# Attention and two mixture-of-experts layers on one core: casts, spare matmuls and scatters moved in a planned order

## Chip, cores and metric

The kernel runs on one core of a Trainium2 chip. The metric is the device time of one execution in microseconds; lower is better. All arithmetic that counts is float32: a matrix is split into a rounded high part and a low part (the rest), and a product is made of three TensorE passes (high by high, high by low, low by high).

## What is computed

```python
def reference(q, k, v, f, moe..., moe2...):         # cut
    scores = q @ k.T / sqrt(64) + decay(cumsum(log f)), causal   # 2 x 8 heads, 576 x 576, head size 64
    x = softmax(scores) @ v                                      # -> 1152 tokens x 512
    # first experts: two modalities, expert = argmax(x @ w_gate + bias[modality]), 8 experts, none dropped
    x = gate * (relu(x @ w1[e]) @ w2[e])                         # 512 -> 1024 -> 512
    # second experts: expert = argmax(x @ w_gate2), at most `capacity` (288) tokens each
    return gate * (relu(x @ w1[e]) @ w2[e])
```

## The kernel before

Nothing is left to a compiler's order. Every step is an `op` of a `Sched` (engine, an estimated duration, a priority, the buffers it reads and writes), and `Sched.run` makes a list schedule from the estimates: it takes whatever can start earliest by the plan, of operations within 0.02 us the one with the least priority, among those whose priority is within a window of the least one that is still to do. Steps marked `fill` (the casts of weights in attention) are put afterwards into gaps of the plan that are long enough. The instructions are then issued in the order of the plan. Each engine works through its own queue strictly in order, and semaphores make it wait for data; so an operation that the plan put too early blocks everything behind it on its engine. The plan's estimates are `PAR` and the numbers in the `op` calls, not the trace.

The stages, with the places that the change touches:

- **Attention**, 16 heads, `head` (L517 on), a planned period of 7.25 us. SP loads q, k and v (`load`, L496). TensorE transposes q and k (L519, L557), makes the scores in groups (L620 to L624), transposes the exponentials (L660), multiplies with v (L693) and turns the result (L717). ScalarE does the exponentials (L642) and the high parts, VectorE the row maxima (L634) and the low parts. Two strings of small VectorE operations, `consts5` (L835 to L843, it ends with a register for SP, which names the first experts to load) and `consts6` (L850 to L868), prepare the routing; each is one `op` with one estimate (0.7 and 1.2 us).
- **First weights**: from the planned time 54.7 us on, SP loads nine chunks of 512 KB (`chunk`, L359) into attention. Of the first four chunks ScalarE makes the high halves (L352) and GpSimd the low halves (L361), as `fill`; the plan lets a cast start when it believes that the load has landed.
- **Idle filler**: `busy` puts up to six matmuls of 128 columns (L1100) ahead of a TensorE operation that is late in the plan, up to the planned time 30 us.
- **First experts**: `route` makes the table of the tokens on VectorE, `tables` the lists, GpSimd gathers rows (L1195). The usual case has two experts of five blocks of 128 tokens. Casts of weights (`Region.split`) are on ScalarE (high) and VectorE (low, L361), and of every 16 low halves two (`plo`) are on GpSimd; four of the eight right after attention (`eplo`) and three of those before the second experts (`eplo2`) are on GpSimd too.
- **Second experts**, `experts()`: for each of the 8 experts a block of 128 tokens, and a second block under `tc.If`, if there are more. Two gathers (L2027) bring the rows, TensorE transposes them (L2035), makes the first product (L2092 to L2094), transposes the hidden layer (L2117), and makes the second product (L2143 to L2145). VectorE scales the result (L2166), GpSimd scatters it to `out` (L2173). Scatters into `out` wait for each other. The scatter of block (0,0) stands on GpSimd's queue ahead of the gathers of expert 1; in the last expert, as in all, block 0 comes ahead of block 1.

Of the kernel before, what the change touches and what calls it, by code (L numbers as in the profile page):

```python
# [13 lines left out]
ALU = mybir.AluOpType  # L14
AX = mybir.AxisListType
# [52 lines left out]
class Sched:  # L68
# [4 lines left out]
    def __init__(self):  # L73
        self.ops, self.slots, self.rings, self.banks = [], {}, 0.0, set()
# [50 lines left out]
    def commit(self, o, t, end):  # L125
# [21 lines left out]
    def run(self, window, slack=0.02, lat=0.18, margin=0.05, free=None, emit=True, busy=None):  # L147
# [11 lines left out]
        while len(order) < len(main):  # L159
# [20 lines left out]
            free[o["eng"]] = t + o["dur"]  # L180
            if busy is not None and o["eng"] == "PE" and t > last:
# [29 lines left out]
        if emit:  # L211
            for t, _, i in order:
                if "idle" in ops[i]:
                    busy(t, *ops[i]["idle"])
                ops[i]["fn"]()
# [8 lines left out]
def kernel(  # L224
# [608 lines left out]

    def consts5():
        vec.tensor_reduce(out=gm, in_=mb, axis=AX.X, op=ALU.max)  # L835
        vec.tensor_tensor(out=ge, in0=mb, in1=gm[:, :, None].to_broadcast([P, 2, E]), op=ALU.is_equal)
        vec.tensor_tensor(
            out=ge, in0=ge, in1=erev[:, :, 0][:, None, :].to_broadcast([P, 2, E]), op=ALU.mult
        )
        vec.tensor_reduce(out=gm, in_=ge, axis=AX.X, op=ALU.max)  # L840
        vec.tensor_tensor(out=go, in0=ge, in1=gm[:, :, None].to_broadcast([P, 2, E]), op=ALU.is_equal)
        vec.tensor_scalar(out=gif, in0=gm, scalar1=-1.0, scalar2=float(E), op0=ALU.mult, op1=ALU.add)
# [5 lines left out]
    def consts6():  # L848

        vec.tensor_tensor(out=g_1, in0=go[:, 0], in1=go[:, 1], op=ALU.mult)  # L850
        vec.tensor_tensor(out=g_1, in0=go[:, 1], in1=g_1, op=ALU.subtract)
        vec.tensor_tensor(out=g_x, in0=go[:, 0], in1=g_1, op=ALU.add)
        vec.tensor_scalar(out=gbig, in0=g_x, scalar1=131072.0, scalar2=None, op0=ALU.mult)
        vec.tensor_scalar(out=g_x, in0=g_x, scalar1=-1.0, scalar2=1.0, op0=ALU.mult, op1=ALU.add)
        vec.tensor_scalar(out=soff, in0=g_x, scalar1=131072.0, scalar2=None, op0=ALU.mult)
        vec.scalar_tensor_tensor(
            out=soff, in0=g_1, scalar=float(NJ * P), in1=soff, op0=ALU.mult, op1=ALU.add
        )
        vec.tensor_copy(out=capf, in_=capi[:, 0:1])
        vec.tensor_scalar(out=capl, in0=capf, scalar1=float(NB2 * P), scalar2=None, op0=ALU.min)  # L860
        vec.tensor_copy(out=idf[:, 1], in_=idi[:, :, 0])
        vec.tensor_scalar(out=idf[:, 0], in0=idf[:, 1], scalar1=-1.0, scalar2=1.0, op0=ALU.mult, op1=ALU.add)
        for m, t in ((0, btok), (1, bt1)):
            vec.tensor_tensor(
                out=t, in0=mb[:, m, :, None].to_broadcast([P, E, TT]),
                in1=idf[:, m, None, :].to_broadcast([P, E, TT]), op=ALU.mult,
            )
        vec.tensor_tensor(out=btok, in0=btok, in1=bt1, op=ALU.add)  # L868
# [165 lines left out]
    a5 = sc.op(D_, 0.7, consts5, prio=c_p0, after=[a1, a4], late=1.0)  # L1034
    a6 = sc.op(D_, 1.2, consts6, prio=c_p0 + T, after=[a3, a5])
# [60 lines left out]
    def busy(t, idle, o):  # L1096

        if t < par["wf1"]:
# [3 lines left out]
    est = sc.run(window=par["window"], free={"SP": 4.1, A_: 6.9, D_: 7.2, "POOL": 5.0}, emit=not par.get("only"), busy=busy)  # L1102
# [60 lines left out]
    class Region:  # L1163


        def __init__(self, two=False):
            self.sc = Sched()
            for n, t in (
                ("h", hps), ("ht", [htps]), ("ht2", [htps, ytps]),
                ("y", yps), ("yl", yps[1:2]), ("y0", yps[0:1]), ("x", [xps, htps] if two else [xps]), ("yt", [ytps]), ("lg", [rps[:, 504:504 + E]]),  # L1170
# [130 lines left out]
        def leave(self, blk, o, dst, second, y=None):  # L1301

            b_l, HD = Buf(None), DM // 2
            if y is not None:
                gate_ = [
                    (A_, 0.27, lambda: nc.scalar.mul(out=o.ap[:, 0:HD], in_=y[:, 0:HD], mul=gsl)),
                    (D_, 0.33, lambda: V.tensor_scalar(
# [5 lines left out]
            if second:  # L1313
# [18 lines left out]
                else:  # L1332
# [3 lines left out]
                    for u, (e, d) in enumerate(((A_, 0.27), (D_, 0.33))):  # L1336
# [105 lines left out]
        def single(self, blk, ie, slot, dst, second, pend=None, half=0, hold=None, deps=(), step=2, u=0, cond=None, later=False):  # L1442
# [5 lines left out]
            use, sb, hts = [], [], "ht" if second else "ht2"  # L1448
# [24 lines left out]
            def turn(i):  # L1473
                t, b = Buf(hts), Buf(None)
# [67 lines left out]
    def route(rg, lgt, pad, eoff, lim, nm, deps=(), shift=None):  # L1542
# [7 lines left out]
        def v(fn, r, dur=0.153, eng=D_):  # L1550
# [265 lines left out]
    rg = Region(True)  # L1816
# [6 lines left out]
    rg.split_load(range(KD, NCH), NCH, plo=par["eplo"])  # L1823
# [185 lines left out]
    def experts():  # L2009
# [11 lines left out]

        def rows(e, u):
# [8 lines left out]
            rg.op("POOL", 1.1, fn, w=[g], late=par["glate"], prio=p_ - 6.0)  # L2031
# [44 lines left out]
        class Block:  # L2076
# [83 lines left out]
            def leave(self, prio, o=None):  # L2160
                blk = bl2[self.e][self.u]
                if o is None:
# [135 lines left out]
```

## Time and profile before

| what | value |
|---|---|
| three timed runs | 495.01, 498.13, 501.61 us (median 498.13) |
| the profiled execution | 497.49 us, of which the span from its first to its last instruction is 495.7 us |
| mean granted TensorE clock | 0.964 of full speed |

The profile's rows come from that one execution. "Busy" is the time in which an engine had an instruction of the program; idle time stands in square brackets with what ended it. The clock column is the TensorE clock that was granted: 1.00 is 2.4 GHz and 0.50 is 1.2 GHz.

### The profile page before, as it was taken

The numbers are of one execution on the slowest core, as the hardware profiler recorded it, in microseconds if no ns is written. First come the engines' busy times: TensorE is split into PE (matmuls) and PEld (weight loads), VectorE is DVE, ScalarE is ACT, GpSimd is POOL, SyncE is SP. The second block draws the span as 40 slices with busy tenths as digits, with TensorE's granted clock in tenths as the row PEclk, the third lists the DMA queues.
The fourth block names the chain that finished last, engine by engine and source line by source line (L and its number), as shares of the span: only waits on it lengthen the run. The fifth ranks groups of instructions, "written<-read, shape, count | busy, mean of one in ns | idle before, by whom it ended". The sixth has DMA issues, their size and how long they took to land. (4 is left out here: it accounts for less than half of the span.)

```text
span 495.7 us, 8168 instructions
## 1 busy us (share of the span) xinstructions
PE 442.6 (89%) x2719; PEld 373.6 (75%) x2719; DVE 320.3 (65%) x684; ACT 270.9 (55%) x602; POOL 157.8 (32%) x190
## 2 busy tenths in 40 slices
PE   7878998899999879999889999897999999999950
PEld 6667887789888777988789977676887678778730
DVE  6797885598896774512771145776656999598320
ACT  6765785798776521502641116356567986497120
POOL 8741312555400512200330005133333283332100
PEclk9998999599999989999999999998999999999995
DMA  7462489997200552411291002417674879550000
GB/s 165 71 142 71 99 137 177 250 285 211 84 24 25 162 214 65 182 53 45 62 306 59 21 23 87 140 50 265 207 242 160 279 247 332 202 196 9 30 23 3
DMA packets 72694, 66.97 MB, mean 135 GB/s; under 512 B 45597, under 2 KB 54813, under 8 KB 72625
## 3 DMA queue, kind: packets, MB, share of 16 engines
q1 hardware_dynamic: 66448, 55.96, 39.3%
q0 software_dynamic: 4992, 10.08, 6.4%
q8 instruction: 25, 0.41, 0.4%
q10 hardware_dynamic: 1200, 0.30, 0.3%
q14 instruction: 29, 0.23, 0.2%
HBM read 58.62 MB, written 11.87 MB: 142 GB/s over the span
## 5 line engine op out<-in xcount | busy, mean ns | idle before, releaser
L2173 POOL DMA_INDIRECT out_dram<-mo,mo x16 | 18.6, 1165 | 79.1 <-DVE mo L2166 41.3
L352 ACT CAST mo<-wb 128x512 fp32r<-128x512 f32 x68 | 39.9, 633 | 4.9 <-PE yps L2145 4.6
L361 DVE TENSOR_TENSOR mo<-wb,mo 128x512 fp32r<-128x512 f32 x53 | 39.7, 777 | 3.8 <-ACT mo L352 3.0
L693 PE MATMUL one<-at,at 128*128 128x64 f32 (+2 forms) x192 | 36.4, 330 | 3.0 <-ACT at L642 1.7
L642 ACT ACTIVATE at<-one,at 128x512 f32<-128x512 f32 (+1 forms) x64 | 33.7, 532 | 8.3 <-DVE at L634 8.1
L352 ACT CAST wa<-wa 128x512 fp32r<-128x512 f32 x56 | 31.8, 623 | 7.8 <-DMA wa<-in_moe_w_dram 7.5
L361 DVE TENSOR_TENSOR wa<-wa,wa 128x512 fp32r<-128x512 f32 x42 | 33.4, 842 | 3.4 <-ACT wa L352 3.4
L693 PEld LDWEIGHTS one<-at,at 128*128 128x128 f32 x192 | 29.3, 194 | 6.5 <-DVE at L671 1.5
L2107 ACT ACTIVATE mo<-hps 128x512 f32<-128x512 f32 x30 | 17.7, 607 | 25.6 <-PE hps L2094 22.1
L671 DVE TENSOR_TENSOR at<-one,at 128x320 fp32r<-128x320 f32 (+1 forms) x32 | 17.6, 556 | 21.0 <-ACT at L667 20.4
L620 PE MATMUL one<-at,at 128*128 128x512 f32 (+1 forms) x64 | 26.6, 417 | 4.2 <-ACT at L709 4.2
L2143 PE MATMUL yps<-mo,wb 128*128 128x512 f32 x72 | 29.0, 402 | 0.6
L2145 PE MATMUL yps<-mo,wb 128*128 128x512 f32 x72 | 28.5, 396 | 0.9 <-DVE wb L2134 0.9
L660 PE MATMUL big<-ident,at 128*128 128x128 f32 x128 | 26.3, 280 | 3.4 <-DVE at L531 3.2
L1351 POOL DMA_INDIRECT x_d<-mo,mo x8 | 8.2, 1024 | 65.4 <-DVE mo L1348 47.8
L2144 PE MATMUL yps<-mo,wb 128*128 128x512 f32 x72 | 28.4, 394 | 0.0
L361 DVE TENSOR_TENSOR mo<-mo,mo 128x512 fp32r<-128x512 f32 x33 | 25.9, 823 | 2.7 <-ACT mo L352 2.7
L634 DVE TENSOR_REDUCE at<-one 128x1 f32<-128x512 f32 (+1 forms) x64 | 27.3, 474 | 0.4 <-PE one L624 0.4
L361 POOL TENSOR_TENSOR mo<-wb,mo 128x512 fp32r<-128x512 f32 x15 | 19.9, 1334 | 19.9 <-ACT mo L352 15.5
L2166 DVE TENSOR_SCALAR mo<-yps,mo 128x512 f32<-128x512 f32 x15 | 11.0, 741 | 23.3 <-PE yps L2145 23.3
L588 POOL TENSOR_TENSOR at<-at,at 128x320 fp32r<-128x320 f32 x16 | 13.9, 870 | 34.0 <-ACT at L577 33.9
L660 PE MATMUL one<-ident,at 128*128 128x128 f32 x112 | 23.4, 281 | 1.4 <-ACT at L642 1.4
(390 smaller groups left out, 1320.5 us busy)
## 6 DMA issues: line engine op xcount, KB each, us to landing
wb<-in_moe_w_dram SPq DMA_DIRECT2D x34, 512.0 KB, 5.2
wa<-in_moe_w_dram SPq DMA_DIRECT2D x28, 512.0 KB, 5.7
mo<-in_moe_w_dram SPq DMA_DIRECT2D x18, 512.0 KB, 5.4
at<-in_q_dram SPq DMA_DIRECT2D x30, 128.0 KB, 4.2
x_d<-zero SPq DMA_DIRECT2D x1, 2340.0 KB, 19.7
at<-in_k_dram SPq DMA_DIRECT2D x16, 128.0 KB, 4.5
at<-in_v_dram SPq DMA_DIRECT2D x16, 128.0 KB, 3.3
x_d<-at SPq DMA_DIRECT2D x8, 256.0 KB, 2.3
```

Source lines behind the costliest of these rows:

```text
L352: nc.scalar.copy(out=half(hi, u), in_=half(rt, u))
L361: lambda u, eng: eng.tensor_tensor(out=half(lo, u), in0=half(rt, u), in1=half(hi, u), op=ALU.subtract),
L620: nc.tensor.matmul(o, q1.ap[:, s0:s0 + n], k1.ap[:, a:e], start=True, stop=False)
L634: nc.vector.tensor_reduce(out=nm.ap[0:n], in_=ps.ap[0:n, c:c + w], axis=AX.X, op=ALU.max, negate=True)
L642: nc.scalar.activation(out=p.ap[0:n, 0:w], in_=ps.ap[0:n, c:c + w], func=AF.Exp, bias=nm.ap[0:n], scale=1.0, accum_out=st.ap[0:n, i:i + 1],)
L660: nc.tensor.transpose(out=t.ap[:, c:c + P], in_=ptile[i].ap[:, j * P:(j + 1) * P], identity=ident)
L693: nc.tensor.matmul(dst.ap[:, qa - off:qb - off], vt.ap[:, j].rearrange("p a d -> p (a d)"), ph[a][u].ap[:, ca:ca + qb - qa], start=(first ...
L2107: nc.scalar.activation(out=self.s.ap[:, 4 * i:4 * i + 4, :], in_=self.h[i].ap.rearrange("p (c t) -> p c t", t=P), func=AF.Relu,)
L2143: nc.tensor.matmul(self.y.ap, a, wh, start=(c == 0), stop=False)
L2144: nc.tensor.matmul(self.y.ap, a, wl, start=False, stop=False)
L2145: nc.tensor.matmul(self.y.ap, b, wh, start=False, stop=(c == KF - 1))
L2173: nc.gpsimd.indirect_dma_start(out=out, out_offset=blk.at(), in_=o.ap[:, 0:DM], in_offset=None, bounds_check=N - 1, oob_is_err=False,)
```

## The change

Six edits. (1) `consts5` and `consts6` become chains of single operations of 0.2 us with later priorities (4 and 5 periods instead of 1 and 2). (2) In the planned times 24 to 42 us, one matmul of 512 columns is put ahead of a TensorE operation whenever 2.4 us have gone by since the last such one. (3) The weight loads in attention count as landing 5 us later in the plan, and their low halves move from GpSimd to VectorE. (4) All other low halves are on VectorE too (`plo`, `eplo`, `eplo2` are empty), and right after attention those of chunks 6 and 7 wait for the list of rows. (5) The first scatter of the second experts waits for the first two gathers. (6) The last expert does its block 1 first and ends with block 0, whose result is scaled in two halves on ScalarE and VectorE. Estimates and offsets of the plan change beside these, and transposes of the hidden layer share two banks with those of the rows.

```diff
@@ Sched.run @@
+            if pace is not None and o["eng"] == "PE" and pace[0] < t < pace[1] and t > self.paced + pace[2]:
+                idle = [s for c in self.banks for s in self.slots[c] if s[2] is None and s[1] + lat < last]
+                if idle:
+                    s = min(idle, key=lambda s: s[1])
+                    self.paced, o["pace"] = t, s[0]
+                    t = max(t, last + 0.22)
...
-                end[o["n"]] = self.rings + 0.95
+                end[o["n"]] = self.rings + 0.95 + o["late"]
@@ attention @@
-    a5 = sc.op(D_, 0.7, consts5, prio=c_p0, after=[a1, a4], late=1.0)
-    a6 = sc.op(D_, 1.2, consts6, prio=c_p0 + T, after=[a3, a5])
+    def chain(steps, prio, after):
+        for fn in steps:
+            after = [sc.op(D_, 0.2, fn, prio=prio, after=after)]
+        return after
+    a5 = sc.op(D_, 0.2, consts5, prio=par["c5"] * T, after=chain(steps5, par["c5"] * T, [a1, a4]), late=1.0)
+    (a6,) = chain(steps6, par["c6"] * T, [a3, a5])
...
             "SP", 0.5, lambda m=m: chunk(m)[0](), w=[lb], after=[a5, a8], dma=1.46, prio=par["w0"] + m * par["w1"],
+            late=par["wlate"],
...
-                sc.op("POOL", 1.2, lambda m=m, u=u: chunk(m)[2](u, nc.gpsimd), r=[hb], fill=True)
+                sc.op(D_, 0.61, lambda m=m, u=u: chunk(m)[2](u, vec), r=[hb], fill=True)
...
     def busy(t, idle, o):
+        if idle is None:
+            nc.tensor.matmul(
+                o[:, 0:512].rearrange("p (a b) -> p a b", b=P), identb, identb[:, None, :].to_broadcast([P, 4, P]),
+                start=True, stop=True,
+            )
@@ first experts @@
-    rg.split_load(range(KD, NCH), NCH, plo=par["eplo"])
+    rg.split_load(range(KD, KD + 2), NCH, plo=())
+    rg.split_load(range(KD + 2, NCH), NCH, plo=(), deps=b_idx.writer)
...
-            use, sb, hts = [], [], "ht" if second else "ht2"
+            use, sb = [], []
...
-                t, b = Buf(hts), Buf(None)
+                t, b = Buf("x"), Buf(None)
@@ second experts @@
-        Block(0, 0, None).leave(-9.0, o)
-        x = {(0, 1): rg.held("X", places[1])}
+        x = {(0, 1): rg.held("X", places[1])}
+        for u in range(2):
+            x[1, u] = rows(1, u)
+        Block(0, 0, None).leave(-4.0, o, after=list(gat))
...
-            b.first_all(p + 0.8)
+            end = e == E - 1
+            b.first_all(p - 0.4 if end else p + 0.8)
...
-            b.second_all(p + 2.2)
-            b.leave(p + 3.0)
+            b.second_all(p + 0.55 if end else p + 2.2)
+            b.leave(p + 0.56 if end else p + 3.0)
+            if end:
+                a.second(0, KF, p + 0.7)
+                a.leave(p + 2.0, two=True)
@@ PAR @@
+    c5=4.0, c6=5.0, pace=(24.0, 42.0, 2.4), wlate=5.0,
-    eplo2=[10, 12, 14], plo=[0, 8], augp=-1.2129, qodd=0.3279,
+    eplo2=[], plo=[], augp=-1.3557, qodd=0.4107,
-    off: 'load': -18.0624, 'T': -11.9995, 'X': 1.5487, 'AV': 2.3039, 'N': 0.0684
+    off: 'load': -20.9527, 'T': -11.5553, 'X': 1.5606, 'AV': 2.8731, 'N': -8.3457
```

## Rows read from the trace of the kernel before

**Rows 1.** The page: busy time of each engine, share, instructions.

```profile
PE 442.6 (89%) x2719; PEld 373.6 (75%) x2719; DVE 320.3 (65%) x684; ACT 270.9 (55%) x602; POOL 157.8 (32%) x190
```

**Rows 2.** Busy time of the engines, and granted clock, in chosen stretches.

```profile
core 0: us, PE busy (x) PEld busy (x) DVE busy (x) ACT busy (x) POOL busy (x), PEclk, DMA share, GB/s
...
40.10:43.50 3.40, 3.16 (x14) 2.67 (x15) 2.20 (x6) 0.98 (x3) 0.00 (x0) 0.50 0.07 17
...
87.90:98.10 10.20, 9.36 (x38) 8.02 (x39) 6.44 (x13) 7.83 (x20) 5.53 (x6) 0.50 0.99 271
100.00:130.00 30.00, 29.86 (x230) 26.07 (x229) 26.38 (x54) 26.87 (x70) 15.56 (x18) 1.00 0.81 229
...
337.00:340.40 3.40, 2.80 (x14) 2.43 (x13) 1.74 (x2) 2.11 (x4) 2.28 (x2) 0.50 1.05 371
340.40:470.00 129.60, 127.35 (x606) 102.02 (x605) 97.56 (x143) 87.28 (x166) 45.46 (x36) 1.00 0.55 189
```

**Rows 3.** Instructions in order of time, VectorE, 22 to 38 us: start, duration.

```profile
22.38 0.16 DVE L835 TENSOR_REDUCE gm<-mb 128x2 f32<-128x16 f32 x1
...
25.47 0.16 DVE L843 CAST gi<-gif 1x2 int32<-1x2 f32 x1
...
33.72 0.15 DVE L850 TENSOR_TENSOR g<-go 128x8 f32<-128x8 f32 x1
...
37.73 0.24 DVE L868 TENSOR_TENSOR at<-at,at 128x80 f32<-128x80 f32 x1
```

**Rows 4.** TensorE in order of time, 24 to 41 us; idle before it in brackets.

```profile
27.33 0.30 PE L660 MATMUL big<-ident,at 128*128 128x128 f32 x1 [2.49 <-DVE at L531]
...
38.69 0.44 PE L620 MATMUL big<-at,at 128*64 128x512 f32 x1 [1.83 <-DVE at L568]
```

**Rows 5.** All engines in order of time, 83 to 89 us.

```profile
83.19 0.40 SPq L359 DMA_DIRECT2D wa<-in_moe_w_dram  x1
...
87.59 0.62 ACT L352 CAST wa<-wa 128x512 fp32r<-128x512 f32 x1 [5.52 <-DMA wa<-in_moe_w_dram]
88.75 0.80 PE L620 MATMUL one<-at,at 128*128 128x512 f32 x1 [4.19 <-ACT at L709]
```

**Rows 6.** The low casts by engine: duration in ns, min/median/max.

```profile
L361 DVE TENSOR_TENSOR mo<-wb,mo x53: 674/680/2268, 168.9 to 460.7; 128x512 fp32r<-128x512 f32 x53
...
L361 POOL TENSOR_TENSOR mo<-wb,mo x15: 1273/1306/1761, 167.5 to 454.0; 128x512 fp32r<-128x512 f32 x15
```

**Rows 7.** In order of time, after attention; last row: same step, second experts' routing.

```profile
167.52 5.57 POOL L361 TENSOR_TENSOR mo<-wb,mo 128x512 fp32r<-128x512 f32 x4 [4.74 <-ACT mo L352]
...
168.85 1.80 DVE L361 TENSOR_TENSOR mo<-wb,mo 128x512 fp32r<-128x512 f32 x1
170.57 1.42 DVE L1571 TENSOR_TENSOR_SCAN mo<-rste,mo 128x80 f32<-128x80 f32 x1
...
176.48 1.77 PE L1008 MATMUL hps<-wb,wa 128*128 128x256 f32 x7 [2.12 <-DVE wb L1021]
...
314.63 0.33 DVE L1571 TENSOR_TENSOR_SCAN mo<-rste,mo 128x80 f32<-128x80 f32 x1
```

**Rows 8.** GpSimd and TensorE in order of time, start of the second experts.

```profile
329.71 1.19 POOL L2173 DMA_INDIRECT out_dram<-mo,mo  x1 [8.37 <-DVE mo L1286]
...
334.23 1.30 POOL L2027 DMA_INDIRECT wb<-x_d,mo  x1 [0.16 <-issue]
...
336.79 0.87 PE L2035 MATMUL xps<-ident,wb 128*128 128x128 f32 x4 [2.55 <-DMA wb<-x_d,mo]
```

**Rows 9.** The end: chain of work that ended last, GpSimd, and two lines' waits.

```profile
479.63 3.28 DMA out_dram<-mo,mo
...
483.68 0.97 POOL L2173 DMA_INDIRECT out_dram<-mo,mo  x1 [3.08 <-DMA out_dram<-mo,mo]
...
L2222 POOLq EVENT_SEMAPHORE  x6: 17/30/43, 486.7 to 487.2; - x6
...
L2222 PEldq COMPARE_BRANCH  x1: 3651/3651/3651, 479.2 to 479.2; - x1
```

More of the change, by code (lines that the diff above doesn't have):

```diff
@@ L73, in __init__ @@
     def __init__(self):
-        self.ops, self.slots, self.rings, self.banks = [], {}, 0.0, set()
+        self.ops, self.slots, self.rings, self.banks, self.paced = [], {}, 0.0, set(), 0.0
     def cls(self, name, aps, bank=False):
@@ L145, in commit, with run @@
         o["at"] = (t, end[o["n"]])
-    def run(self, window, slack=0.02, lat=0.18, margin=0.05, free=None, emit=True, busy=None):
+    def run(self, window, slack=0.02, lat=0.18, margin=0.05, free=None, emit=True, busy=None, pace=None):
         ops = self.ops
@@ L214, in run @@
                     busy(t, *ops[i]["idle"])
+                if "pace" in ops[i]:
+                    busy(t, None, ops[i]["pace"])
                 ops[i]["fn"]()
@@ L846, in consts5 @@
         )
[L848 to L856, printed above, removed]
-            out=soff, in0=g_1, scalar=float(NJ * P), in1=soff, op0=ALU.mult, op1=ALU.add
[L858 to L868, printed above, removed]
@@ L1096, in busy @@
     def busy(t, idle, o):
-        if t < par["wf1"]:
+        if idle is None:
[3 more added lines that the diff above has]
+            )
+        elif t < par["wf1"]:
             for _ in range(min(par["wfn"], int((idle - par["wfm"]) / 0.055))):
                 nc.tensor.matmul(o[:, 0:P], identb, identb, start=True, stop=True)
-    est = sc.run(window=par["window"], free={"SP": 4.1, A_: 6.9, D_: 7.2, "POOL": 5.0}, emit=not par.get("only"), busy=busy)
+    est = sc.run(window=par["window"], free={"SP": 4.1, A_: 6.9, D_: 7.2, "POOL": 5.0}, emit=not par.get("only"), busy=busy,
+                 pace=par["pace"])
     if par.get("only"):
@@ L2030, in fn @@
                 )
-            rg.op("POOL", 1.1, fn, w=[g], late=par["glate"], prio=p_ - 6.0)
+            gat.append(rg.op("POOL", 1.1, fn, w=[g], late=par["glate"], prio=p_ - 6.0))
             def fn():
@@ L2158, in second_all, with leave @@
                 uses(ms, rg.op("PE", par["dur1"], fn, r=[self.d] + self.hb + ready(ms), w=[self.y], prio=prio))
-            def leave(self, prio, o=None):
+            def leave(self, prio, o=None, two=False, after=()):
                 blk = bl2[self.e][self.u]
-                if o is None:
+                if two:
+                    o, g = Buf("yo"), blk.gs[:, blk.col:blk.col + 1]
+                    HD = DM // 2
+                    for eng, fn in (
+                        (A_, lambda: nc.scalar.mul(out=o.ap[:, 0:HD], in_=self.y.ap[:, 0:HD], mul=g)),
+                        (D_, lambda: V.tensor_scalar(
+                            out=o.ap[:, HD:DM], in0=self.y.ap[:, HD:DM], scalar1=g, scalar2=None, op0=ALU.mult)),
+                    ):
+                        rg.op(eng, 0.4, fn, r=[self.y], w=[o], prio=prio)
+                elif o is None:
                     o = Buf("yo")
@@ L2176, in fn @@
                     )
-                rg.op("POOL", 1.1, fn, r=[o], late=2.2, prio=prio + 0.5)
+                rg.op("POOL", 1.1, fn, r=[o], late=2.2, prio=prio + 0.5, after=after)
+        x = {(0, 1): rg.held("X", places[1])}
+        for u in range(2):
+            x[1, u] = rows(1, u)
         o = Buf(None)
         o.ap = ys[2]
-        Block(0, 0, None).leave(-9.0, o)
-        x = {(0, 1): rg.held("X", places[1])}
+        Block(0, 0, None).leave(-4.0, o, after=list(gat))
         for m in range(3 * NCH, 3 * NCH + KD):
@@ L2201, in experts @@
             b = Block(e, 1, x[e, 1], n_e[e])
-            b.first_all(p + 0.8)
-            b.relu(0, p + 0.9)
-            b.relu(1, p + 0.9)
-            if e > 0:
+            end = e == E - 1
+            b.first_all(p - 0.4 if end else p + 0.8)
+            b.relu(0, p - 0.3 if end else p + 0.9)
+            b.relu(1, p - 0.3 if end else p + 0.9)
+            if e > 0 and not end:
                 a.second(0, 4, p + 0.7)
-            b.turn([0, 1], p + 1.2)
-            if e > 0:
+            b.turn([0, 1], p + 0.35 if end else p + 1.2)
+            if e > 0 and not end:
                 a.second(4, KF, p + 1.3)
                 a.leave(p + 2.0)
-                if e + 1 < E:
-                    for k in range(KD):
-                        weights(NCH * (e + 3) + k, p + 3.0 + k)
-            b.second_all(p + 2.2)
-            b.leave(p + 3.0)
+                for k in range(KD):
+                    weights(NCH * (e + 3) + k, p + 3.0 + k)
+            b.second_all(p + 0.55 if end else p + 2.2)
[3 more added lines that the diff above has]
+                a.leave(p + 2.0, two=True)
         rg.run()
```

69 lines of the change are left out of this document (47 added, 22 removed).

## Prediction

> **What bounds the kernel now.** I read the busy times first [rows 1]: TensorE is busy for 442.6 of 495.7 us, no other engine for more than 65%. So the end moves only where TensorE waits, or where it works at the lower clock. I then cut the span into stretches of one microsecond and looked for those with little TensorE work or a clock under 1.00. Apart from start and end there are few. The clock stands at 0.50 (1.2 GHz) in five places, and each follows a hole in TensorE's work: 3.4 us in early attention, 10.2 us in mid attention, 3.4 us at the start of the second experts [rows 2], and two more stretches of 3.4 us like these, right after attention and in the second routing. At that level a matmul takes twice as long, so a stretch costs half its length where TensorE is busy throughout: 1.7 us, 5.1 us. What made each hole is read in the order of time.
>
> Early attention: TensorE waits for VectorE 2.49 us and 1.83 us [rows 4]. VectorE at that time works through `consts5`, from 22.38 to 25.63, and `consts6`, from 33.72 to 37.97 [rows 3]; the plan has 0.7 and 1.2 us for them, and the low parts that TensorE needs are queued behind.
>
> Mid attention: ScalarE stands 5.52 us ahead of a weight cast, whose load was issued only at 83.19. Behind the cast stands the copy that frees a bank for TensorE, which waits 4.19 us [rows 5] and then works at 1.2 GHz for 10.2 us.
>
> After attention: TensorE waits 2.12 us for VectorE. In that stretch GpSimd runs four low casts, and VectorE's operations are stretched beside them: a cast takes 1.80 us, a scan 1.42 us that takes 0.33 us in the second routing, where GpSimd has no cast [rows 7].
>
> Second experts: GpSimd stands 8.37 us ahead of the first scatter, with both gathers of expert 1 behind it; TensorE then waits 2.55 us for the first gathered rows [rows 8].
>
> End: the last scatter that carries rows lands at 482.91, a second one, of the last expert's block 1, is issued behind it at 483.68, and GpSimd's final wait is over at 486.7 [rows 9].
>
> **The change part by part**, against the profiled execution's 497.49 us (495.7 us of span and 1.8 us around it), which lies 0.64 us below the median of the runs.
>
> *Strings of small operations.* The work on VectorE stays; what goes is the block of 3.25 us and of 4.25 us in one piece. At most the two waits and the slow stretch vanish: 2.49 + 1.83 + 1.7 = 6.0 us. Against it: the 21 operations still cost VectorE at least 0.15 us each [rows 3], 3.2 us, in a stage where it is nearly full. I put half of them on the path, 1.6 us. The spare matmuls are 18 / 2.4 = 7 at most, of 0.21 us (127.35 us / 606 [rows 2]), 1.5 us. Most follow an operation after which TensorE waits anyway, and that wait hides them; with the waits gone they are on the path. I take half, 0.7 us. Each also needs a bank that the plan, not the chip, knows to be free; if a reader is late, TensorE waits behind it. Sum 6.0 - 1.6 - 0.7 = 3.7 us, ends 0 and 6.0. Nothing on SP is gained or lost as long as the register for SP is written when SP gets there: its load stands in SP's queue with the q, k and v loads behind it. It costs at most the lag of VectorE, and the whole string took 3.25 us.
>
> *Casts 5 us later.* ScalarE waited 5.52 us, so a place 5 us later leaves 0.5 us. The copy then runs at once, and the 4.19 us and the 5.1 us of the slow stretch go with the wait: 9.3 us at most. The reloads behind the low casts move later on SP too; they fetch weights for the second product of the second expert, far behind, which hides that. What is late next is VectorE: eight low casts of 0.68 us [rows 6] come to it, 5.4 us, where it is busy 26.38 of 30 us and ScalarE 26.87 [rows 2], so there is room for 3.6 us in 30. They go into gaps of the plan; I put half on the path, 2.7 us, ends 0 and 5.4. Sum 9.3 - 0.5 - 2.7 = 6.1 us, ends 0 and 9.3.
>
> Here a rule speaks against the change. In this trace a low cast on VectorE beside one on GpSimd takes up to 2.27 us instead of 0.68 [rows 6]. The Trainium skill (SBUF — State Buffer, "Who interferes with whom") says that a VectorE instruction with two SBUF inputs contends with a GpSimd instruction that reads SBUF, and that the loser blocks fully; the trace agrees. The other VectorE steps of attention take one input from PSUM, the moved casts take both from SBUF, so by this rule the casts would now collide with GpSimd's own steps of attention. By the stretch that the rows show, 1.6 us, for every one of the eight casts, that would be 12.8 us more on VectorE; it is part of the last rival below.
>
> *Low casts after attention.* Before the list is ready VectorE has four of its own, as now; the other four come after it. The stretches go: 1.80 - 0.68 = 1.1 us and 1.42 - 0.33 = 1.1 us on these two rows alone [rows 6, 7], which is as much as TensorE's wait. So 2.12 us goes, and 1.7 us for the slow stretch behind it: 3.8 us at most. The casts of chunks 6 and 7 are hidden by the first half of the second product. I take 3.5, ends 0 and 3.8.
>
> *Low casts elsewhere.* GpSimd has 32 low casts in three rows of that view, of which one stands [rows 6]: 8 in attention, 4 right after it, 20 later. These 20 cost VectorE 20 x 0.68 = 13.6 us. But each GpSimd cast held a VectorE cast for up to 1.6 us; from both sides this is between 14 us more and 18 us less of VectorE's time, and VectorE is busy only 97.56 of 129.6 us in the second experts [rows 2]. I take 0.
>
> *First scatter.* The gathers go ahead of it, so the second leaves GpSimd by 329.71, where the scatter now starts, instead of at 335.5 [rows 8], and their rows are there when TensorE asks. Nothing waits for that scatter but the next one. 2.55 us and 1.7 us: 4.25 at most, I take 4.0; ends 0 and 4.3.
>
> *Last expert.* The empty scatter goes ahead, so the end hangs on the scatter with rows, landing at 482.91, or on TensorE's last branch, which ends at 479.2 + 3.65 = 482.9 [rows 9], in place of 486.7: 3.8 us. The halved scaling can't bring the end ahead of that branch. I take 3.7, ends 2 and 3.8.
>
> *Offsets, estimates and shared banks* have no row that prices them: 0, with 2 us either way.
>
> Sum: 3.7 + 6.1 + 3.5 + 4.0 + 3.7 = 21.0 us. 497.5 - 21.0 = 476.5, or 477 beside the median of the runs. With every part at its upper end it is 6.0 + 9.3 + 3.8 + 4.3 + 3.8 = 27.2 us, 470, and 468 with the offsets' 2 us.
>
> **The rivals.** *Attention gives nothing.* The stalls there come of a plan that is ahead of the chip. If SP's queue is held up just as before and the weight load is issued later by as much as the cast, ScalarE stops ahead of it again; and if VectorE is full, the deferred strings stop TensorE elsewhere. For it: VectorE is 88% busy later on [rows 2]. Against it: only the cast is moved, and nothing of it moves the load. Then 3.5 + 4.0 + 3.7 = 11.2 us are left: 498.1 - 11.2 = 487, with 2 us either way.
>
> *The later stages give nothing*: the gathers find no free buffer, or TensorE waits for VectorE after attention although GpSimd is quiet. Only attention's 9.8 us and the end's 3.7 us are left, 485.
>
> *VectorE becomes the bound*, the slower side. Place: attention from 85 us on and the second experts. Price: all 32 moved casts on the path, 32 x 0.68 = 21.8 us, and the eight in attention also held by GpSimd, 12.8 us: 34.6 us. Against the 21.0 us (with the 2.7 us counted already) that is 11 us more than now, 509. It decides from the point where VectorE's share in these stretches reaches 1; now it is 0.88 and 0.75 [rows 2], which speaks against it.
>
> **How the numbers follow.** My forecast, all five parts within their ends, has 0.64, with a range of its own of 468 to 485; attention without gain 0.20; later stages without gain 0.10; VectorE as the bound 0.06. The time is the forecast's, 477. The range takes in the two middle cases up to 489, and 467 below: it leaves out the last rival and some of the edges. 2% of 498.1 is 10 us, about what a measurement of this kernel can tell from no change, so faster by over 2% means under 488.2: the forecast, most of the third case and over half of the second, 0.83; slower 0.04; the rest, 0.13, lies within.
>
> **What would show it.** Right: no stretch at 0.50 between 80 and 100 us, no wait of ScalarE for a weight load over 1 us, no VectorE cast over 0.8 us outside attention, the gathers of expert 1 ahead of the first scatter, one scatter in the last 10 us. Wrong: VectorE full and TensorE waiting for it from 85 us on; a wait of SP for the register of `consts5`, with loads behind it; a slow stretch in early attention in spite of the spare matmuls. The prediction fails most easily in attention, where a new order is planned on estimates that the chip doesn't keep.

## The result, and the profile after

The changed kernel takes 476.53 us (median of four executions, 475.46 to 482.73); the kernel before, run beside it, takes 498.77 (495.01 to 501.61). The ratio is 0.956, 95% interval 0.949 to 0.963: faster, by 22 us. Measured again as the control of the experiments it took 475.85 us (468.65 to 476.46), ratio 0.947 (0.937 to 0.957). Medians take in every execution; ratios leave out those more than 1.5% above the fastest of their kernel. The rows of after below come from an execution of that second measurement that took 476.46 us, with a span of 474.6 us.

The page, busy time of each engine, to be held against [rows 1]:

```profile
PE 438.7 (92%) x2730; PEld 370.6 (78%) x2730; DVE 315.6 (66%) x716; ACT 270.1 (57%) x603; POOL 115.9 (24%) x158
```

TensorE has lost 4 us of busy time and 17 us of idle time. VectorE has 32 instructions more and is busy 5 us less, GpSimd 42 us less.

Busy times and clock by stretch, columns as in [rows 2]:

```profile
22.60:26.00 3.40, 3.40 (x14) 2.64 (x13) 2.53 (x4) 1.93 (x8) 3.22 (x10) 0.51 0.54 97
92.00:122.00 30.00, 30.00 (x228) 26.42 (x228) 27.71 (x59) 27.22 (x73) 8.45 (x10) 1.00 0.93 254
128.40:135.20 6.80, 6.80 (x33) 6.30 (x33) 4.69 (x13) 3.49 (x11) 0.00 (x0) 0.50 0.15 43
312.70:316.10 3.40, 3.40 (x9) 2.64 (x8) 3.30 (x8) 3.38 (x7) 2.13 (x3) 0.50 0.40 111
323.00:452.60 129.60, 125.63 (x592) 100.03 (x591) 94.22 (x154) 87.28 (x167) 30.45 (x23) 1.00 0.57 193
```

The stretches at 0.50 near 40, 88, 177 and 337 us are gone; one in the second routing stays (320 us before, 313 now), and two are new, at 22.6 and 128.4. The second row answers to the one from 100 to 130 of before: VectorE is busy 27.71 of 30 us where it was 26.38, and TensorE is not held up by it: 30.00 of 30. (The window ends ahead of the wait at 126.67, whose cause is another, see below.) In the second experts (last row) VectorE is busy less than before, 94.22 us against 97.56, with more instructions.

All engines in order of time (start, duration; idle before in brackets):

```profile
45.44 0.13 DVE L845 TENSOR_REDUCE gm<-mb 128x2 f32<-128x16 f32 x1
...
55.38 0.73 DVE L863 TENSOR_TENSOR g<-go 128x8 f32<-128x8 f32 x1
...
57.90 0.44 PE L630 MATMUL one<-at,at 128*128 128x384 f32 x1 [1.25 <-DVE at L681]
...
63.91 0.24 DVE L883 TENSOR_TENSOR at<-at,at 128x80 f32<-128x80 f32 x1
...
84.11 0.36 SPq L369 DMA_DIRECT2D wa<-in_moe_w_dram  x1
86.84 2.25 POOL L555 TENSOR_TENSOR at<-at,one_c 64x576 fp32r<-64x576 f32 x2 [2.74 <-ACT at L537]
88.23 1.72 DVE L732 TENSOR_SCALAR at<-at 128x5 f32<-128x5 f32 x1
89.06 0.86 POOL L598 TENSOR_TENSOR at<-at,at 128x320 fp32r<-128x320 f32 x1
90.53 0.63 ACT L362 CAST wa<-wa 128x512 fp32r<-128x512 f32 x1
91.00 0.44 PE L630 MATMUL big<-at,at 128*64 128x512 f32 x1 [1.30 <-DVE at L541]
...
121.04 0.67 DVE L371 TENSOR_TENSOR wa<-wa,wa 128x512 fp32r<-128x512 f32 x1
121.39 2.44 POOL L555 TENSOR_TENSOR at<-at,one_c 64x576 fp32r<-64x576 f32 x2 [2.72 <-ACT at L537]
122.78 2.84 DVE L732 TENSOR_SCALAR at<-at 128x5 f32<-128x5 f32 x1
123.80 0.85 POOL L598 TENSOR_TENSOR at<-at,at 128x320 fp32r<-128x320 f32 x1
124.60 0.99 POOL L908 MEMSET wb<- 128x520 f32 x2
125.65 0.19 DVE L735 RECIPROCAL at<-at 128x5 f32<-128x5 f32 x1
125.86 0.76 DVE L541 TENSOR_TENSOR at<-big,at 64x576 fp32r<-64x576 f32 x1
126.67 0.45 PE L630 MATMUL big<-at,at 128*64 128x512 f32 x1 [2.43 <-DVE at L541]
...
164.21 0.31 DVE L1598 TENSOR_TENSOR_SCAN mo<-rste,mo 128x80 f32<-128x80 f32 x1
...
313.04 1.00 POOL L2057 DMA_INDIRECT wb<-x_d,mo  x1 [0.30 <-issue]
314.34 1.10 POOL L2213 DMA_INDIRECT out_dram<-mo,mo  x1 [0.30 <-issue]
319.62 0.60 PE L2065 MATMUL xps<-ident,wb 128*128 128x128 f32 x4
...
456.77 0.98 POOL L2213 DMA_INDIRECT out_dram<-mo,mo  x1 [7.24 <-DVE mo L2206]
462.86 0.98 POOL L2213 DMA_INDIRECT out_dram<-mo,mo  x1 [5.11 <-DVE mo L2198]
```

Against the rows of before: the strings' operations now lie spread from 45.44 to 64.15 us, and the two waits of [rows 4] are gone. One of 1.25 us has come in their place: at 57.90 TensorE waits for a VectorE step (L681) that stands behind seven operations of the second string, L863 to L869, from 55.38 to 57.32 us. The weight load is issued at 84.11, hardly later than the 83.19 of [rows 5], but its cast stands at 90.53 and nothing waits for it. The scan after attention takes 0.31 us, no longer 1.42 [rows 7]. Both gathers are ahead of the first scatter, which waits for nothing, and TensorE finds its gathered rows at 319.62 without a wait [rows 8]. The last scatter is the one that carries rows, ready when VectorE has scaled them [rows 9].

New are the rows from 86.84 to 91.00 and from 121.39 to 126.67. An addition of 128x5 elements, L732, takes 1.72 and 2.84 us and ends when GpSimd falls idle; behind it in VectorE's order stands the subtraction (L541) for which TensorE waits 1.30 and 2.43 us. The forecast has no term for either.

The groups by form (duration in ns, min/median/max), to be held against [rows 6], with the addition and GpSimd's last wait:

```profile
L371 DVE TENSOR_TENSOR mo<-wb,mo x68: 657/683/693, 162.8 to 442.1; 128x512 fp32r<-128x512 f32 x68
L371 DVE TENSOR_TENSOR wa<-wa,wa x56: 650/684/693, 98.2 to 433.0; 128x512 fp32r<-128x512 f32 x56
...
L732 DVE TENSOR_SCALAR at<-at x16: 151/172/2842, 16.6 to 150.8; 128x5 f32<-128x5 f32 x16
...
L2267 POOLq EVENT_SEMAPHORE  x6: 17/30/43, 465.7 to 466.2; - x6
```

No low cast is stretched any more: the longest takes 693 ns where the first of these groups had 2268. The addition's median is 0.17 us. GpSimd's final waits begin at 465.7 us, 8.9 us ahead of the end; before it was 486.7 [rows 9], 9.0 us ahead, so what was gained at the end was gained before them.

**The span by stage.** Four instants are found in each trace: the first hidden product of the first experts (A; it follows attention), their first second product (B), the first product of the second experts (C), the end.

| kernel | start to A | A to B | B to C | C to end | span |
|---|---|---|---|---|---|
| before | 166.97 | 17.47 | 144.04 | 167.22 | 495.70 |
| changed | 161.86 | 12.51 | 138.01 | 162.24 | 474.62 |
| difference | -5.1 | -5.0 | -6.0 | -5.0 | -21.1 |

Where nothing behind A was edited, A to B and B to C agree within 0.2 us in all traces of the experiments, so these columns can tell more than the whole times. The first and last columns don't repeat so well: in the six traces whose attention is the changed kernel's, A comes at 156.15 to 166.99 us, and where nothing behind A was edited, C to end takes 159.7 to 165.3. So the -5.1 and the last -5.0 are one execution against one. The columns spread because the clock falls behind different holes in different executions: in the changed kernel's first profiled execution, of 482.73 us, the slow stretches stood at 91 and 128 us and, in the second experts, at 316 and 395; in the one shown here at 22, 128 and 313. That is the changed kernel's spread from 468.65 to 482.73 us.

### The profile page after: what moved, and what is told of

It reads as the page before. It is cut to its first block, busy times and chain, and to the rows that moved or that the text cites. A ratio compares the mean times of both kernels' runs of the same rounds, so it can differ in the third digit from the quotient of the medians.

```text
span 480.9 us, 8157 instructions
## 1 busy us (share of the span) xinstructions
PE 443.8 (92%) x2730; PEld 374.8 (78%) x2730; DVE 316.2 (66%) x716; ACT 270.8 (56%) x603; POOL 115.8 (24%) x158
## 4 chain that ended last, share of the span: by engine, by line
PE 49%; issue 22%; DMA 9%; DVE 6%; ACT 6%; POOL 5%; POOLq 1%; ACTq 0%
DMA out_dram<-mo,mo 9%; PE hps L1443 7%; PE one L703 5%; PE yps L1391 4%; PE yps L1393 4%; PE yps L1392 4%; PE one L727 3%; PE hps L1023 3%; PE one L630 2%; DVE at L681 2%; ACT at L652 2%; PE big L567 2%; POOL wb L2057 2%; PE rps L1368 2%; PE one L670 2%
## 5 line engine op out<-in xcount | busy, mean ns | idle before, releaser
L371 DVE TENSOR_TENSOR mo<-wb,mo 128x512 fp32r<-128x512 f32 x68 | 44.1, 684 | 4.4 <-ACT mo L362 4.4
L371 DVE TENSOR_TENSOR wa<-wa,wa 128x512 fp32r<-128x512 f32 x56 | 35.4, 682 | 7.2 <-ACT wa L362 7.2
L703 PE MATMUL one<-at,at 128*128 128x64 f32 (+2 forms) x192 | 37.7, 336 | 2.0 <-DVE at L681 1.3
L681 DVE TENSOR_TENSOR at<-one,at 128x320 fp32r<-128x320 f32 (+1 forms) x32 | 17.2, 555 | 11.4 <-ACT at L677 11.0
L598 POOL TENSOR_TENSOR at<-at,at 128x320 fp32r<-128x320 f32 x16 | 14.2, 889 | 43.1 <-ACT at L587 43.0
L371 DVE TENSOR_TENSOR mo<-mo,mo 128x512 fp32r<-128x512 f32 x36 | 23.5, 683 | 0.4 <-ACT mo L362 0.4
L1353 ACT COPY mo<-ytps 128x512 f32<-128x512 f32 (+1 forms) x10 | 5.7, 567 | 32.1 <-PE ytps L1346 32.1
L670 PE MATMUL one<-ident,at 128*128 128x128 f32 x112 | 22.4, 275 | 1.1 <-ACT at L652 0.9
```

The source lines that it names most:

```text
L371: lambda u, eng: eng.tensor_tensor(out=half(lo, u), in0=half(rt, u), in1=half(hi, u), op=ALU.subtract),
L670: nc.tensor.transpose(out=t.ap[:, c:c + P], in_=ptile[i].ap[:, j * P:(j + 1) * P], identity=ident)
L681: nc.vector.tensor_tensor(out=lo.ap, in0=t.ap[:, 0:width], in1=hi.ap, op=ALU.subtract)
L703: nc.tensor.matmul(dst.ap[:, qa - off:qb - off], vt.ap[:, j].rearrange("p a d -> p (a d)"), ph[a][u].ap[:, ca:ca + qb - qa], start=(first ...
```

## The experiments

All are edits of the changed kernel unless said otherwise, and compared with its 475.85 us; the runs of before beside them had medians of 497.44 to 498.48 us.

**c_after**, the changed kernel itself.

> The changed kernel itself, as the base for the other runs here. Both theories: 474 to 479 us, about 22 us below the kernel before. Its profile should show no stretch at a clock of 0.50 between 80 and 100 us if the cast's 5 us did what the forecast says; the slow execution first profiled had one at 91 us, behind a wait of 1.3 us.

475.85 us. No stretch at 0.50 between 80 and 100 us here, but the hole at 91 us is there, 1.30 us long, and a longer one at 126.67.

**u_wlate**: only the weight casts at their old time.

```
-  plo=[], wlate=5.0,
+  plo=[], wlate=0.0,
```

> Only the 5 us on the weight casts are taken back; the order of the main operations in attention stays. Forecast's theory (the cast blocked ScalarE, its wait cost a bank and the clock): ScalarE waits about 5 us for a load again, a stretch at 0.50 follows, and the time is 6 us above the changed kernel (up to 9.3), about 483. Rival (attention gained nothing, the rest gained more): within 1.5 us of the changed kernel, and no wait of ScalarE for a load over 1 us.

483.40 us (478.10 to 486.25), 7.5 us above the changed kernel. In order of time, ScalarE and TensorE:

```profile
89.61 0.62 ACT L362 CAST wa<-wa 128x512 fp32r<-128x512 f32 x1 [7.38 <-DMA wa<-in_moe_w_dram]
...
91.01 1.33 PE L567 MATMUL big<-ident,at 128*128 128x128 f32 x5 [6.21 <-ACT at L652]
```

The cast's wait is back, and the clock stands at 0.50 for 10.2 us there. The output product of head 7 comes at 100.97 instead of 93.64, 7.3 us later; that of head 5, ahead of the cast, comes at 75.66 instead of 75.22, so 6.9 us arise here. The rival falls: the load's place is the same, only the cast had moved.

**u_pace**: no spare matmuls.

```
-                 pace=par["pace"])
+                 pace=None)
```

> The changed kernel without the spare matmuls. Theory A (they cost only their own time, the strings removed the holes): 0.7 us faster than the changed kernel, within 1.5, and no slow stretch in early attention. Theory B (they are what keeps the clock up there): a stretch of 3.4 us at 0.50 comes back between 25 and 45 us, and the time is 1 to 2 us above the changed kernel.

475.63 us (468.34 to 480.46): no difference. The trace shows no slow stretch between 20 and 60 us without them. The chip ran seven of them in the changed kernel, of 0.38 to 0.63 us each by their rows, 2.9 us in all. Theory A is the nearer, but its 0.7 us can't be seen; that they keep the clock up is not shown.

**u_chain**: the two strings as blocks at the old places.

```
-    a5 = sc.op(D_, 0.2, consts5, prio=par["c5"] * T, after=chain(steps5, par["c5"] * T, [a1, a4]), late=1.0)
-    (a6,) = chain(steps6, par["c6"] * T, [a3, a5])
+    a5 = sc.op(D_, 0.7, lambda: [fn() for fn in steps5 + [consts5]], prio=c_p0, after=[a1, a4], late=1.0)
+    a6 = sc.op(D_, 1.2, lambda: [fn() for fn in steps6], prio=c_p0 + T, after=[a3, a5])
```

> The two strings of small VectorE operations as two blocks again, at the places of the kernel before; all else as changed. Forecast: 3.7 us slower than the changed kernel (0 to 6.0), TensorE's waits of 2.5 and 1.8 us for VectorE back between 22 and 40 us. Rival (the spare matmuls did it, the strings nothing): the waits are back but not the slow stretch, and the time is within 1.5 us of the changed kernel since later waits take up the lag.

480.06 us (474.46 to 482.73), 4.2 us above the changed kernel; A comes at 165.14, 3.3 us later. VectorE and TensorE in order of time:

```profile
38.23 0.84 DVE L883 TENSOR_TENSOR at<-at,at 128x80 f32<-128x80 f32 x1
38.99 0.74 DVE L578 SCALAR_TENSOR_TENSOR at<-big,at 64x576 fp32r<-64x576 f32 x1
...
39.88 0.45 PE L670 MATMUL big<-ident,at 128*128 128x128 f32 x1 [3.27 <-DVE at L578]
```

One wait of 3.27 us in the place of the two expected, and a stretch of 3.4 us at 0.50 from 39 us on, spare matmuls or not. It was the strings.

**u_pool**: the low casts outside attention back on GpSimd.

```
-    rg.split_load(range(KD, KD + 2), NCH, plo=())
-    rg.split_load(range(KD + 2, NCH), NCH, plo=(), deps=b_idx.writer)
+    rg.split_load(range(KD, NCH), NCH, plo=par["eplo"])
-  eplo2=[], ... plo=[],
+  eplo2=[10, 12, 14], ... plo=[0, 8],
```

> All low casts after attention back on GpSimd where the kernel before had them (four right after attention, twenty later); attention, the order of the gathers and the end stay as changed. Forecast: 3.5 us (0 to 3.8) slower than the changed kernel, all of it between the last product of attention and the first second-product, where the slow stretch of 3.4 us comes back; nothing from there to the end of the first experts (0, from 14 faster to 18 slower). Rival, from the landmarks of the two traces (that later stretch is 8.8 us shorter in the changed kernel): 10 to 12 us slower, with VectorE's casts stretched over 1.5 us and TensorE waiting for them in the first experts.

481.96 us (476.25 to 488.81), 6.1 us above the changed kernel. A to B is 18.69 us instead of 12.51, B to C 140.19 instead of 138.01, C to end 159.43, the shortest of all. (A, at 156.15 us, is early because this execution met no slow stretch in attention.) In order of time after attention:

```profile
156.70 5.55 POOL L371 TENSOR_TENSOR mo<-wb,mo 128x512 fp32r<-128x512 f32 x4 [4.75 <-ACT mo L362]
158.03 1.79 DVE L371 TENSOR_TENSOR mo<-wb,mo 128x512 fp32r<-128x512 f32 x1
159.74 1.42 DVE L1598 TENSOR_TENSOR_SCAN mo<-rste,mo 128x80 f32<-128x80 f32 x1
...
166.11 4.21 PE L1023 MATMUL hps<-wb,wa 128*128 128x256 f32 x18 [2.47 <-DVE wb L1036]
```

VectorE's cast and the scan are stretched as in [rows 7], TensorE waits 2.47 us and works 6.8 us at 0.50. The mechanism is the forecast's, but worth 6.2 us, not 3.5. 2.2 us more come, in B to C, from casts that were put at nothing: 1.0 us near 237 us, where GpSimd has casts at 231.30 and 237.60, and 1.1 us near 299 us, just behind the three that stand ahead of the second experts (293.03 to 297.27). The rival's 10 to 12 us are too many. The run takes back, together with the casts, the wait of those of chunks 6 and 7 for the list, so these two are not told apart.

**u_poolattn**: the eight low casts inside attention back on GpSimd.

```
-    sc.op(D_, 0.61, lambda m=m, u=u: chunk(m)[2](u, vec), r=[hb], fill=True)
+    sc.op("POOL", 1.2, lambda m=m, u=u: chunk(m)[2](u, nc.gpsimd), r=[hb], fill=True)
```

> Only the eight low casts inside attention back on GpSimd. Forecast: they cost VectorE 5.4 us there, of which 2.7 were put on the path, so 2.7 us faster than the changed kernel (0 to 5.4). Rival (VectorE has room, and GpSimd's cast stretches VectorE's operations beside it): 0 to 3 us slower, with VectorE's operations of attention longer by up to 1.6 us beside each of the eight.

475.56 us (474.46 to 478.03): no difference. VectorE has room for them, as the row from 92 to 122 us shows, and neither theory's price is paid.

**u_gather**: the first scatter ahead of the gathers.

```
+        o = Buf(None)
+        o.ap = ys[2]
+        Block(0, 0, None).leave(-9.0, o)
         for u in range(2):
             x[1, u] = rows(1, u)
-        o = Buf(None)
-        o.ap = ys[2]
-        Block(0, 0, None).leave(-4.0, o, after=list(gat))
```

> Only the first scatter of the second experts ahead of the gathers again. Forecast: 4.0 us slower than the changed kernel (0 to 4.3): GpSimd stands some 8 us ahead of the scatter, TensorE waits about 2.5 us for the first gathered rows and a stretch of 3.4 us at 0.50 follows. Rival (the gathers wait for something else by now): within 1 us.

482.85 us (477.12 to 486.54), 7.0 us above the changed kernel. In the profiled execution 5.1 us of that arise in attention, where no instruction differs (slow stretches at 93 and 130 us); C to end is 166.60 us instead of 162.24, 4.4 us more. GpSimd and TensorE in order of time:

```profile
319.33 1.20 POOL L2213 DMA_INDIRECT out_dram<-mo,mo  x1 [5.83 <-DVE mo L1313]
320.83 1.53 POOL L2057 DMA_INDIRECT wb<-x_d,mo  x1 [0.30 <-PE hps L2124]
...
326.10 1.08 PE L2065 MATMUL xps<-ident,wb 128*128 128x128 f32 x4 [2.79 <-DMA wb<-x_d,mo]
```

The wait is back with its slow stretch, 3.4 us from 325 us on: 2.79 + 1.7 = 4.5 us, near the forecast's 4.0. That the last column has about the same is chance: c_after lost 1.7 us at 313 that this run didn't, and from 388 to 401 us, where both wait for rows, this run falls back by another 1.2 us. Against u_pace, which has no slow stretch behind C, TensorE falls back by 4.7 us at this place, and 4.1 of them are left at 386 us.

**u_last**: the last expert in the old order.

```
-            end = e == E - 1
+            end = False
-                for k in range(KD):
+                for k in range(KD if e + 1 < E else 0):
```

> Only the last expert in the order of before, its first block ahead of its second. Forecast: 3.7 us slower than the changed kernel (2 to 3.8), all of it behind the last product: a second scatter issued behind the landing of the one with rows, and GpSimd's final wait some 17 us after TensorE's last product, in place of 13. Rival (the end hangs on TensorE's branches): within 1 us.

482.24 us (479.35 to 482.46), 6.4 us above; again 5.0 us of the profiled execution's 6.0 arise in attention. GpSimd at the end:

```profile
464.70 0.98 POOL L2213 DMA_INDIRECT out_dram<-mo,mo  x1 [10.01 <-DVE mo L2206]
468.86 0.98 POOL L2213 DMA_INDIRECT out_dram<-mo,mo  x1 [3.19 <-DMA out_dram<-mo,mo]
```

The second scatter is back, and from the last product to the end it is 16.97 us instead of 13.07. C to end, though, is only 1.05 us longer. The control had a slow stretch in it that this run lacks (1.7 us, at 313) and 2.03 us of waiting near 390 us against 1.79; with these it is 1.05 + 1.7 + 0.24 = 3.0 us. Against the other traces with the new end, their slow stretches taken off in the same way, it is 0.9 to 3.6 us. So the tail gained 3.9 us, and about 0.9 of it went into TensorE's last products.

**u_banks**: the PSUM classes of the experts' transposes as before.

```
-  ("y0", yps[0:1]), ("x", [xps, htps]),
+  ("ht", [htps]), ("ht2", [htps, ytps]), ("y0", yps[0:1]), ("x", [xps, htps] if two else [xps]),
-  t, b = Buf("x"), Buf(None)
+  t, b = Buf(hts), Buf(None)
```

> The changed kernel with the PSUM classes of the experts' transposes as before (first experts: x transposes in one bank, transposes of the hidden rows in two others; second routing: two banks for x), all else as changed. Forecast: 0 (the shared banks were put at nothing, 2 us either way with the offsets). Rival (the 6 us that the stretch of second products of the first experts is shorter come from the banks as much as from the low casts): 2 to 4 us slower, TensorE waiting over 1 us for VectorE to empty the one x bank near 239 us, as in the kernel before.

475.70 us (469.55 to 480.45): no difference in the times. B to C is 139.37 us, 1.4 more, which is one wait, in order of time:

```profile
234.22 0.66 PE L1230 MATMUL xps<-ident,wb 128*128 128x128 f32 x4 [1.40 <-DVE mo L1242]
```

So the banks gave 1.4 us that the forecast did not have, less than the rival's 2 to 4.

**later_only**: attention of before, all behind it as changed.

```
(u_chain, u_poolattn and u_wlate together, pace=None, and the offsets of before)
```

> Attention as in the kernel before (strings as blocks, weight casts early, no spare matmuls, its eight low casts on GpSimd, old offsets), all that lies behind attention as changed. Forecast: the later parts are worth 3.5 + 4.0 + 3.7 = 11.2 us, so 487. From the landmarks of the changed kernel's traces (the stretch from the first hidden product to the end is 15.9 us shorter): 482. Rival that attention gained nothing: the time of the changed kernel, 476.

482.24 us (480.62 to 484.05), ratio to before 0.972 (0.966 to 0.977): the later parts are worth 16.0 us, attention 6.4. That is the time read from the stages, not the forecast's 487. In its trace A comes at 166.68 us, as before, with before's slow stretch:

```profile
87.80:98.00 10.20, 9.52 (x40) 8.36 (x41) 6.44 (x13) 8.08 (x20) 5.79 (x6) 0.50 1.02 275
```

**u_offs**: attention's offsets (`off`, `qodd`, `augp`) of before.

```
-  'load': -20.9527, 'T': -11.5553, ... 'X': 1.5606, ... 'AV': 2.8731, ... 'N': -8.3457
+  'load': -18.0624, 'T': -11.9995, ... 'X': 1.5487, ... 'AV': 2.3039, ... 'N': 0.0684
```

> The changed kernel with attention's offsets of before (when each step of a head is due); all else as changed. Forecast: 0, 2 us either way. Theory A (the new due time of the row sums' additions puts them beside GpSimd's copies, so the change gave back what it had gained): the waits of 1.30 and 2.43 us near 90 and 126 us go, 3 to 8 us faster than the changed kernel. Theory B (the offsets are what gives attention its gain): slower by 2 us or more, TensorE waiting for VectorE elsewhere in attention.

473.02 us (470.89 to 475.42), 2.8 us below the changed kernel, but within the spread of its executions (468.65 to 482.73), so the time alone doesn't show a gain. The addition, by form:

```profile
L732 DVE TENSOR_SCALAR at<-at x16: 153/172/1145, 18.0 to 145.8; 128x5 f32<-128x5 f32 x16
```

With its due time `N` (moved by the change from 0.07 to -8.35 us) the longest is 1.15 us instead of 2.84, and TensorE's waits of 1.30 and 2.43 us are gone; one of 1.82 us for ScalarE comes instead, at 83.71. A comes at 156.79 us, 5.1 us ahead of c_after's, which is half of the 10.2 us that c_after's attention has at 0.50 and this one hasn't; u_pool, with the changed offsets and no such stretch, had 156.15. So what is to be gained lies in the clock. The waits are theory A's, the time is short of its lower end.

**noadd**: the reciprocal straight from the row sums.

```
-            nc.vector.tensor_scalar(
-                out=rs.ap[:, :, 0], in0=st.ap, scalar1=1e-9, scalar2=None, op0=ALU.add
-            )
-            nc.vector.reciprocal(out=rs.ap, in_=rs.ap)
+            nc.vector.reciprocal(out=rs.ap[:, :, 0], in_=st.ap)
```

> The changed kernel, with the reciprocal of the softmax row sums taken straight from the sums: the 16 additions of 1e-9 ahead of it (a row sum is at least 1, since the row's own maximum gives exp(0)) are left out; the order of all else stays. Theory A (these additions, 128x5 from SBUF to SBUF, stand until GpSimd is idle: 1.72 us at 88.23 and 2.84 us at 122.78 in the changed kernel, 0.17 us alone; TensorE's waits of 1.30 and 2.43 us and the slow stretches behind them hang on them): both waits and the stretches near 91 and 128 us go, the time is 4 to 9 us below the changed kernel, about 470, and it varies less. Theory B (the reciprocal stands there just as long, or TensorE waits for what VectorE does next): within 1.5 us of the changed kernel.

467.03 us (six executions, 466.29 to 468.64), ratio to before 0.941 (0.936 to 0.945), and 8.8 us below the changed kernel. Its slowest execution is where the fastest of the changed kernel's nine is. In order of time:

```profile
85.03 2.25 POOL L555 TENSOR_TENSOR at<-at,one_c 64x576 fp32r<-64x576 f32 x2 [2.74 <-ACT at L537]
86.40 0.19 DVE L732 RECIPROCAL at<-at 128x5 f32<-128x5 f32 x1
...
87.64 0.48 PE L630 MATMUL big<-at,at 128*64 128x512 f32 x1
...
117.99 2.45 POOL L555 TENSOR_TENSOR at<-at,one_c 64x576 fp32r<-64x576 f32 x2 [2.71 <-ACT at L537]
119.36 0.19 DVE L732 RECIPROCAL at<-at 128x5 f32<-128x5 f32 x1
...
120.59 0.48 PE L630 MATMUL big<-at,at 128*64 128x512 f32 x1
```

and by stretch:

```profile
82.00:112.00 30.00, 29.54 (x227) 26.22 (x226) 27.46 (x58) 29.06 (x77) 9.83 (x12) 1.00 0.96 266
112.00:142.00 30.00, 28.80 (x220) 25.03 (x218) 26.22 (x66) 23.65 (x65) 6.18 (x8) 1.00 0.29 95
```

The reciprocal takes 0.19 us in the midst of GpSimd's copies, TensorE waits for neither subtraction, and the clock stays at 1.00 throughout attention. A comes at 152.65 us instead of 161.86: 1.30 + 2.43 us of waits and half of the 10.2 us at 0.50 are 8.8 of these 9.2 us. The 1.7 us of the stretch at 22.6 are not the additions' doing: the waits of TensorE ahead of it (1.59, 0.31 and 0.57 us from 20 to 22 us) are in this run too, and the clock didn't fall. Against u_pool, whose attention has the additions and no slow stretch, A is 3.5 us earlier; so much is left of the waits themselves, and the rest is the clock behind them. Theory A. This kernel beats both.

## Why the prediction came true, and where it was wrong

The time is within 0.5 us of the forecast, and each of the five parts did what its mechanism said. But that the sum came so near is luck, since two errors cancel: attention gave 6.4 us by later_only (5.1 between the two executions shown), not 9.8, and the rest 16.0, not 11.2. Point by point:

- *Strings*: 3.7 us forecast, 4.2 by undoing them (3.3 at A). Right. Of the 1.6 us put on the path 1.25 show, at 57.90. The spare matmuls took 2.9 us, not the 1.5 that an average matmul's time gave, and the 0.7 us put on the path are not to be seen.
- *Casts 5 us later*: 6.1 forecast, 7.5 measured (6.9 in the trace). Of the 2.7 us that the forecast took off for the eight low casts nothing is paid: putting them on GpSimd changes no time.
- *Low casts after attention*: 3.5 forecast and 3.8 as its upper end, 5.0 from before to after, 6.2 when undone. The term was sized by the wait that ends last, 2.12 us, and one slow stretch; the smaller waits of TensorE ahead of it in the routing (0.32 and 0.62 us in the trace of before) went too.
- *Low casts elsewhere*: 0 forecast, 2.2 us measured ahead of the second experts. In the second experts the casts on GpSimd cost nothing that shows (C to end is 159.43 us in u_pool).
- *First scatter*: 4.0 forecast, 4.1 to 4.7 us where the edit acts. Right.
- *Last expert*: 3.7 forecast, the tail 3.9 us shorter, about 3.0 of it left (0.9 to 3.6). The row that the forecast read as the end of GpSimd's final wait is the start of it, 9.0 us ahead of the end; as that distance stayed (8.9 us), the term came right.
- *Offsets, estimates and shared banks*: "0, with 2 us either way". This is the step that failed. The banks gave 1.4 us. With the new offsets the row sums' addition stands up to 2.84 us, with those of before up to 1.15 (u_offs), and without it 8.8 us are had (noadd). What the offsets cost by themselves is not settled: the 2.8 us of u_offs lie within the spread, and only the whole set was taken back, not the offset `N` alone. The forecast had no row for it, but the trace of before has: there the same addition (L722) takes up to 0.95 us, median 0.17, and each of the five over 0.25 us lies beside a GpSimd step. Its stretch could have been priced as that of the casts was.

What stood between the attention that was forecast and the one measured is thus for the most part shown: without the addition A comes 14.3 us ahead of the kernel before, more than the forecast's 9.8. Not all of it is the change's, as the kernel before has its additions too.

Of the signs that the forecast named for itself, those for the casts, the gathers and the end are there. Of the signs against it two are seen: a slow stretch in early attention, at 22.6, which begins ahead of the first spare matmul (24.97), and TensorE waiting for VectorE behind 85 us, though VectorE isn't full. And while c_after has no stretch at 0.50 between 80 and 100 us, the execution of 482.73 us has one at 91, behind the addition's wait.

The rivals fall: attention does give something (later_only is 6.4 us slower than the changed kernel), the later stages give more than their part, and VectorE is at 0.92 in mid attention and 0.73 in the second experts without being the bound.

The rule drawn on, the Trainium skill's SBUF — State Buffer, "Who interferes with whom", was right and I applied it to the wrong instructions. I looked at the low casts, with two SBUF inputs, and wrote that the other VectorE steps of attention take one input from PSUM; the addition (L732) takes its only input from SBUF. None of the casts is stretched in the changed kernel; the one at 121.04 was issued ahead of GpSimd's copy, took its 0.67 us, and the copy pair took 2.44 instead of 2.25. The same section names a second kind, single-input copies, casts and `tensor_scalar` in a two-port mode, and says that whoever issues first has the pair of SBUF ports that VectorE and GpSimd share for the whole instruction while the other blocks. The addition is a `tensor_scalar` from SBUF to SBUF, and its two long ones here were begun inside GpSimd's copies; the trace agrees, with 2.84 us against 0.17.

Left open: noadd with the offsets of before was not tried; the offset `N` was not moved alone. Of the 6.0 us of B to C 2.2 and 1.4 are shown by undoing; the slow stretch of the second routing, which lay ahead of C before and lies behind it now, can hold at most 1.7, and the rest has no run.

## What to carry to other kernels

When steps are given new places, list what each of them will lie beside, the tiny ones too: here a 0.17 us operation on five columns stood for as long as GpSimd was busy, and what it cost was the work queued behind it and the clock after the hole. Price terms by stages that repeat to 0.2 us, since whole times of one kernel differed by 14 us with where the clock happened to fall; and a stage that doesn't repeat needs several traces. A total that comes out right doesn't show that its terms were: undo each part alone.

## What the runs showed of the hardware

- The addition of 122.78 us stood through three kinds of GpSimd step in a row (a copy, L598, the memsets L908) and ended 0.03 us after the last of them, at 125.62. The one of 88.23 us ended 0.03 us after a copy and L598. So here it didn't wait for one instruction but until GpSimd left a gap; the section of the Trainium skill named above speaks of the one instruction that holds the pair, and the measurement goes beyond it.
- A RECIPROCAL of the same shape, also from SBUF to SBUF, took 0.19 us beside GpSimd's copies.
- In ten profiled executions with TensorE's wait of about 2.4 us near 126 us, the clock fell to 0.50 (1.2 GHz) behind it in nine, for 6.8 or 10.2 us, and not in the tenth (u_pool). Behind the wait of 1.3 us near 91 us it fell in three of nine, and behind one of 1.25 us near 58 us in one of eight (u_banks). The same order of instructions therefore has several times.
